# Reading two stages of matmul passes backwards, and changing the order of the three passes in two others

## The chip, the cores and the metric

One core of one Trainium2 chip runs the whole program. The metric is the device time of one execution in microseconds (us). The profile is a trace of one execution, on the five engines: TensorE (PE; its loads of the stationary operand are listed apart as PEld), VectorE (DVE), ScalarE (ACT), GpSimd (POOL) and SyncE (SP, which here only issues DMAs).

## What is computed

```python
scores = scale * q @ k^T - log(S)          # 4 batches, 12 heads, S = 448, head size 64
x = sigmoid(scores) @ v                    # joined to 1792 tokens x 768
x = square(relu(x @ moe_w_in)) @ moe_w_out # 768 -> 2048 -> 768
h = x @ moe2_w_in
out = (h * sigmoid(1.702 * h)) @ moe2_w_out
```

All inputs and outputs are float32.

## The kernel before

The program has an attention part (the first 128 us of the span) and then eight stages of one kind, in which the two feed-forward layers are computed. A stage is one of the four weight matrices for one half of the tokens: STAGES lists them as (layer, in or out, half), and stages 0, 1, 4, 5 multiply by an "in" matrix, stages 2, 3, 6, 7 by an "out" matrix. Every matrix product is done by a Strassen scheme of seven products P1 to P7, each cut into 8 units, so a stage has 56 units (UNITS) and the program 448.

A unit is three steps of [128 x 128] stationary by [128 x 448] moving (the list `pairs` in `product`). For accuracy each float32 operand is held as a high part and a low rest, both in the type fp32r, and a step is three matmuls ("passes") into one PSUM bank: high weights by high data (line 475), high weights by the rest of the data (line 476), low weights by high data (line 477). The weights are the stationary operand (tiles `s`, three of them in turn: `sh` is the high part, `lo` the low one), the data the moving one (tiles `t`: index 0 the high part, index 1 the rest). A stage thus has 56 x 3 x 3 = 504 passes, the eight stages 4032.

ACT writes the high parts of the weights (`s<-ld`, for two units at a time) and of the data (`t<-...`), DVE the low ones from them. SP brings the weight blocks from DRAM into `ld`. ACT and DVE also move finished PSUM banks out, and prepare the Strassen sums. The order of the instructions on every engine comes from a planner in the program: units on PE stand in a fixed order, the rest is placed by due times. The planner counts a unit as a whole (UNIT_US) and doesn't look into `go`, the function in `product` that issues the passes of one unit.

Each matmul instruction carries its own load of the stationary operand; the trace shows one load for every pass.

Of the kernel before, what the change touches and what calls it, by code (L numbers as in the profile page):

```python
# [16 lines left out]
B, H, S, D = 4, 12, 448, 64  # L17
# [15 lines left out]
UNITS = 7 * NF  # L33
# [44 lines left out]
WINDOW, URGENT = 0.25, 3.0  # L78

PACE = (6, 6, 5, 1, 4, 5, 5)  # L80


@with_exitstack
def sigmoid_attention_two_ffn(ctx: ExitStack, tc: tile.TileContext, qk, v, w, outT):
# [3 lines left out]
    nc = tc.nc  # L88
# [28 lines left out]
    mem = {"ps": ppool.tile([P, 8, 512], F32, name="ps")}  # L117
# [155 lines left out]
    turn, count = [0], [0]  # L273
# [190 lines left out]
    def product(unit, pairs, ready):  # L464
        sl = SL[unit // 2 % NSLOT]

        def go():
            sh, lo = sl[:, 0, unit % 2], sl[:, 1, unit % 2]
            if unit == 0:
                one = [nc.const_aps.tensor(1.0, [P, n], mybir.dt.bfloat16) for n in (P, D)]  # L470
                nc.tensor.matmul(mem["ps"][:, pairs[0][0], :D], *one, start=True, stop=True)  # L471
            for b, c, t, k, start, stop in pairs:
                cols = slice(c * P, (c + 1) * P)
                o = mem["ps"][:, b, :S]
                nc.tensor.matmul(o, sh[:, cols], t[:, 0, k], start=start, stop=False, skip_group_check=True)  # L475
                nc.tensor.matmul(o, sh[:, cols], t[:, 1, k], start=False, stop=False, skip_group_check=True)  # L476
                nc.tensor.matmul(o, lo[:, cols], t[:, 0, k], start=False, stop=stop, skip_group_check=True)  # L477

        units[unit].fn = go
        units[unit].need(lows[unit // 2], ready)  # L480
        for b in {b for b, *_ in pairs}:
            units[unit].need(*held.pop(b, ()))
# [181 lines left out]
    def settle():  # L664
# [16 lines left out]
        assert len(order) == len(Node.all)  # L681
        marks = [(0, 0.0), (PACE[0], pe_at[units[0]])]
        for st, count in enumerate(PACE[1:]):
            marks.append((marks[-1][0] + count, pe_at[units[(st + 1) * UNITS]]))
# [184 lines left out]
```

## Time and profile before

| | |
|---|---|
| Three timed runs | 951.08 us median, 950.97 to 951.43 |
| The profiled execution | 950.77 us, of which the span from first to last instruction is 949.0 us |
| PE, PEld, DVE, ACT busy | 100%, 87%, 85%, 64% of the span |
| Granted TensorE clock, mean | 1.000 |
| The 1344 passes of each of lines 475, 476, 477 | 29% of the chain that ended last, each |

A pass is listed with about 365 ns, though the next begins about 0.2 us after it: passes overlap in the array and their ends are modelled, so that the distance between two starts is what a pass costs, not its listed duration.

### The profile page before, as it was taken

To read this page: it belongs to the slowest core of one execution; us is meant where nothing else is said; L and a number is where in the kernel's file an instruction comes from. 1 tells how busy PE (TensorE), PEld (TensorE's weight loads), DVE (VectorE), ACT (ScalarE), POOL (GpSimd) and SP (SyncE) were. 2 spreads that over 40 slices of the span, in tenths; PEclk is the share of its full clock that TensorE was granted. 3 is DMA by queue.
4 is the path that set the end of the run, shared out by engine and by line. 5 is a ranking of instruction groups with operands and counts; after the bars stand their busy time and mean duration, and the time that the engine had idled before them with its cause. 6 is when DMAs were issued, how large, how long until landed. Compare 5 with 4: busy or idle time off the path is not lost.

```text
span 949.0 us, 13696 instructions
## 1 busy us (share of the span) xinstructions
PE 944.6 (100%) x4949; PEld 822.8 (87%) x4949; DVE 809.3 (85%) x839; ACT 604.6 (64%) x715; POOL 53.5 (6%) x100
## 2 busy tenths in 40 slices
PE   9999999999999999999999999999999999999998
PEld 4555479999999999999999999999999999999997
DVE  3989986699877999999999987999989999778662
ACT  6788776778868775555464666657684646445551
POOL 0110100000000000000000000000000000000000
PEclk9999999999999999999999999999999999999999
DMA  8899989999886766896567699877975448754341
GB/s 340 301 335 356 335 293 332 324 354 334 290 324 227 250 231 212 317 364 216 161 243 286 202 359 325 312 247 251 351 279 171 133 146 288 261 166 132 115 137 58
DMA packets 98627, 245.75 MB, mean 259 GB/s; under 512 B 10752, under 2 KB 72960, under 8 KB 94464
## 3 DMA queue, kind: packets, MB, share of 16 engines
q1 hardware_dynamic: 84736, 150.51, 46.5%
q0 software_dynamic: 13824, 94.38, 27.2%
q8 instruction: 38, 0.62, 0.3%
q14 instruction: 29, 0.24, 0.1%
HBM read 175.11 MB, written 69.73 MB: 258 GB/s over the span
## 4 chain that ended last, share of the span: by engine, by line
PE 100%; ACT 0%; issue 0%
PE ps L475 29%; PE ps L476 29%; PE ps L477 29%; PE ps L332 6%; PE ps L298 5%; PE ps L346 1%; PE ps L317 1%; PE ps L790 0%; PE ps L293 0%; ACT xq L635 0%; PE ps L471 0%
## 5 line engine op out<-in xcount | busy, mean ns | idle before, releaser
L475 PE MATMUL ps<-t,s 128*128 128x448 f32 x1344 | 490.9, 365 | 0.0
L477 PE MATMUL ps<-t,s 128*128 128x448 f32 x1344 | 490.8, 365 | 0.0
L476 PE MATMUL ps<-t,s 128*128 128x448 f32 x1344 | 490.8, 365 | 0.0
L153 ACT ACTIVATE s<-ld 128x768 fp32r<-128x768 f32 x224 | 189.4, 846 | 249.4 <-PE ps L476 206.6
L477 PEld LDWEIGHTS ps<-t,s 128*128 128x128 f32 x1344 | 252.5, 188 | 19.9
L476 PEld LDWEIGHTS ps<-t,s 128*128 128x128 f32 x1344 | 252.5, 188 | 19.9
L475 PEld LDWEIGHTS ps<-t,s 128*128 128x128 f32 x1344 | 252.5, 188 | 19.9
L156 DVE TENSOR_TENSOR s<-ld,s 128x768 fp32r<-128x768 f32 x224 | 213.6, 954 | 61.7 <-ACT s L153 56.6
L156 DVE TENSOR_TENSOR t<-h,t 128x1344 fp32r<-128x1344 f32 (+1 forms) x72 | 100.4, 1397 | 8.8 <-ACT t L153 8.7
L153 ACT ACTIVATE t<-h 128x1344 fp32r<-128x1344 f32 (+1 forms) x72 | 85.6, 1190 | 4.4 <-DVE h L156 2.9
L153 ACT ACTIVATE h<-ps 128x448 f32<-128x448 f32 x112 | 59.8, 536 | 27.0 <-PE ps L477 26.8
L153 ACT ACTIVATE a<-ps,bias 128x896 f32<-128x896 f32 x72 | 66.1, 1023 | 3.2 <-PE ps L293 3.2
L332 PE MATMUL ps<-a,rv 128*64 128x448 f32 x288 | 56.8, 543 | 0.1
L217 DVE SCALAR_TENSOR_TENSOR dec<-raw,dec 128x1536 uint32<-128x1536 uint32 x32 | 56.2, 1755 | 0.5
L219 DVE SCALAR_TENSOR_TENSOR dec<-raw,dec 128x1536 uint32<-128x1536 uint32 x32 | 56.1, 1753 | 0.3
L153 ACT ACTIVATE dec<-raw 128x1536 f32<-128x1536 f32 x32 | 51.9, 1621 | 0.0
L156 DVE TENSOR_TENSOR h<-h,h 128x1344 f32<-128x1344 f32 (+1 forms) x36 | 50.0, 1397 | 1.0 <-DMA h<-hm 0.8
L153 ACT ACTIVATE h<-h 128x896 f32<-128x896 f32 x48 | 44.9, 945 | 4.8 <-DVE h L156 4.4
L332 PEld LDWEIGHTS ps<-a,rv 128*64 128x64 f32 x288 | 19.6, 137 | 32.4 <-issue 22.6
L213 DVE TENSOR_SCALAR dec<-dec 128x1536 f32<-128x1536 f32 x32 | 30.7, 959 | 15.6 <-ACT dec L153 15.6
L156 DVE TENSOR_TENSOR t<-xq,t 128x1344 fp32r<-128x1344 f32 x24 | 37.2, 1552 | 5.9 <-ACT t L153 5.4
L156 DVE TENSOR_TENSOR h<-ps,h 128x448 f32<-128x448 f32 x64 | 38.8, 619 | 2.8 <-PE ps L477 2.5
(58 smaller groups left out, 616.1 us busy)
## 6 DMA issues: line engine op xcount, KB each, us to landing
ld<-scr SPq DMA_DIRECT2D x448, 192.0 KB, 3.8
raw<-in_w POOLq DMA_DIRECT2D x32, 1536.0 KB, 8.2
scr<-dec POOLq DMA_DIRECT2D x32, 768.0 KB, 5.5
scr<-raw POOLq DMA_DIRECT2D x28, 576.0 KB, 6.2
hm<-h SPq DMA_DIRECT2D x32, 448.0 KB, 5.8
h<-hm SPq DMA_DIRECT2D x16, 672.0 KB, 5.4
rq<-in_qk SPq DMA_DIRECT2D x22, 448.0 KB, 8.2
rv<-in_v SPq DMA_DIRECT2D x12, 448.0 KB, 6.1
```

The lines of the kernel that those rows point to most:

```text
L153: nc.scalar.activation(out, in_, fn, **kw)
L156: nc.vector.tensor_tensor(out=out, in0=in0, in1=in1, op=op)
L213: dve(lambda: nc.vector.tensor_scalar(out=d, in0=d, scalar1=LEAST, scalar2=LARGEST, op0=ALU.max, op1=ALU.min), 4 * W, [dk], each=0.52e-3)
L217: dve(lambda: nc.vector.scalar_tensor_tensor(out=u, in0=raw[:, :, 0], scalar=29, in1=u, op0=ALU.logical_shift_right, op1=ALU.bitwise_or), ...
L219: dve(lambda: nc.vector.scalar_tensor_tensor(out=u, in0=raw[:, :, 1], scalar=0x80000000, in1=u, op0=ALU.bitwise_and, op1=ALU.bitwise_or), ...
L298: nc.tensor.matmul(ps[:, j, :S], kk[rows, keys], qq[rows, QUERIES], start=(i == 0), stop=(i == 2))
L317: nc.tensor.matmul(ps[out, j, :S], r[rows, :LEFT], r[rows, QUERIES], start=True, stop=True)
L332: nc.tensor.matmul(ps[rows, :S], t[:, hp % 2 * NFULL + c, rows], a[:, j], start=(c == 0), stop=False)
L346: nc.tensor.matmul(mem["ps"][out, b + i, :S], t[rows, 2 * NFULL, out], AL[rows, j], start=False, stop=True)
L475: nc.tensor.matmul(o, sh[:, cols], t[:, 0, k], start=start, stop=False, skip_group_check=True)
L476: nc.tensor.matmul(o, sh[:, cols], t[:, 1, k], start=False, stop=False, skip_group_check=True)
L477: nc.tensor.matmul(o, lo[:, cols], t[:, 0, k], start=False, stop=stop, skip_group_check=True)
```

## The change

In `product`, stages 1 and 2 (TURNED: an "in" stage and an "out" stage) read the 448 columns of the moving operand from the last to the first, and write the 448 columns of the PSUM bank from the last to the first too. Each column of data still lands in its own column of the bank; all passes of these two stages are turned alike. In stages 4 and 5 (SWAPPED, both "in" stages) the third pass stands in second place: high by high, low weights by high data, high weights by the rest. The sums are the same but for the order of addition.

```diff
 PACE = (6, 6, 5, 1, 4, 5, 5)
+
+TURNED, SWAPPED = (1, 2), (4, 5)
...
+            turn = -1 if unit // UNITS in TURNED else 1
+
             for b, c, t, k, start, stop in pairs:
                 cols = slice(c * P, (c + 1) * P)
-                o = mem["ps"][:, b, :S]
-                nc.tensor.matmul(o, sh[:, cols], t[:, 0, k], start=start, stop=False, skip_group_check=True)
-                nc.tensor.matmul(o, sh[:, cols], t[:, 1, k], start=False, stop=False, skip_group_check=True)
-                nc.tensor.matmul(o, lo[:, cols], t[:, 0, k], start=False, stop=stop, skip_group_check=True)
+                o = mem["ps"][:, b, :S][:, ::turn]
+                hi, rest = t[:, 0, k][:, ::turn], t[:, 1, k][:, ::turn]
+                passes = [(sh, hi), (sh, rest), (lo, hi)]
+                if unit // UNITS in SWAPPED:
+                    passes = [passes[i] for i in (0, 2, 1)]
+                for i, (a, x) in enumerate(passes):
+                    nc.tensor.matmul(o, a[:, cols], x, start=start and i == 0, stop=stop and i == 2, skip_group_check=True)
```

On DVE, ACT, POOL and SP the instructions stand in the same order as before. On PE the same number of passes works on the same tiles; all of them now have one line, 484, and rows that read alike are drawn together with a count.

PE at the start of stage 4 (the first of the swapped ones), before. The names are the PSUM tile `ps`, the data tile `t` and the weight tile `s`, and in brackets stands the engine whose semaphore a pass waits for:

```order
L475 MATMUL ps_149<-t1_107,s1_116 128x448 [waits Activation_49]
L476 MATMUL ps_149<-t1_107,s1_116 128x448 [waits DVE_49]
L477 MATMUL ps_149<-t1_107,s1_116 128x448 [waits DVE_49]
L475 MATMUL ps_149<-t1_107,s1_116 128x448
L476 MATMUL ps_149<-t1_107,s1_116 128x448
L477 MATMUL ps_149<-t1_107,s1_116 128x448
```

The same place after:

```order
L484 MATMUL ps_149<-t1_107,s1_116 128x448 [waits Activation_49]
L484 MATMUL ps_149<-t1_107,s1_116 128x448 [waits DVE_49]
L484 MATMUL ps_149<-t1_107,s1_116 128x448 x16
L484 MATMUL ps_149<-t2_108,s2_117 128x448 [waits Activation_49]
L484 MATMUL ps_149<-t2_108,s2_117 128x448 [waits DVE_49]
L484 MATMUL ps_149<-t2_108,s2_117 128x448 x7
```

Before, the second pass waited for the rest of the data and the third for the low weights; now the second pass of a fresh weight tile waits for the low weights, and no wait stands at the third.

PE at the start of stage 1 (the first of the turned ones), before:

```order
L475 MATMUL ps_149<-t2_108,s1_116 128x448 [waits Activation_49]
L476 MATMUL ps_149<-t2_108,s1_116 128x448
L477 MATMUL ps_149<-t2_108,s1_116 128x448 [waits DVE_49]
L475 MATMUL ps_149<-t2_108,s1_116 128x448
L476 MATMUL ps_149<-t2_108,s1_116 128x448
```

The same place after:

```order
L484 MATMUL ps_149<-t2_108,s1_116 128x448 [waits Activation_49]
L484 MATMUL ps_149<-t2_108,s1_116 128x448
L484 MATMUL ps_149<-t2_108,s1_116 128x448 [waits DVE_49]
L484 MATMUL ps_149<-t2_108,s1_116 128x448 x6
L484 MATMUL ps_149<-t2_108,s1_116 128x448 [waits DVE_49]
```

Nothing moved here: the waits stand at the same passes, and the direction of the columns doesn't show in such rows.

## Rows read from the trace of the kernel before

**Rows 1.** The page: busy time of PE and PEld, share, instructions; granted clock.

```profile
PE 944.6 (100%) x4949; PEld 822.8 (87%) x4949; DVE 809.3 (85%) x839; ACT 604.6 (64%) x715; POOL 53.5 (6%) x100
...
PEclk9999999999999999999999999999999999999999
```

**Rows 2.** The page: the chain of work that ended last, by engine and line.

```profile
PE 100%; ACT 0%; issue 0%
PE ps L475 29%; PE ps L476 29%; PE ps L477 29%; PE ps L332 6%; PE ps L298 5%; PE ps L346 1%; PE ps L317 1%; PE ps L790 0%; PE ps L293 0%; ACT xq L635 0%; PE ps L471 0%
```

**Rows 3.** Groups by line: busy us, mean ns; idle us before them, who ended it.

```profile
L475 PE MATMUL ps<-t,s 128*128 128x448 f32 x1344 | 490.9, 365 | 0.0
L477 PE MATMUL ps<-t,s 128*128 128x448 f32 x1344 | 490.8, 365 | 0.0
L476 PE MATMUL ps<-t,s 128*128 128x448 f32 x1344 | 490.8, 365 | 0.0
L475 PEld LDWEIGHTS ps<-t,s 128*128 128x128 f32 x1344 | 252.5, 188 | 19.9
L476 PEld LDWEIGHTS ps<-t,s 128*128 128x128 f32 x1344 | 252.5, 188 | 19.9
L477 PEld LDWEIGHTS ps<-t,s 128*128 128x128 f32 x1344 | 252.5, 188 | 19.9
```

**Rows 4.** Stretches by stage, 0 to 7: busy us (instructions) by engine, clock, DMA.

```profile
core 0: us, PE busy (x) PEld busy (x) DVE busy (x) ACT busy (x) POOL busy (x), PEclk, DMA share, GB/s
128.06:230.28 102.22, 102.22 (x509) 94.76 (x506) 83.74 (x92) 72.11 (x97) 8.75 (x16) 1.00 0.93 329
230.28:332.42 102.14, 102.14 (x505) 94.68 (x504) 86.33 (x97) 79.67 (x106) 8.70 (x16) 1.00 0.78 277
332.42:434.57 102.15, 102.15 (x505) 94.68 (x504) 99.33 (x93) 59.85 (x62) 3.74 (x7) 1.00 0.81 286
434.57:536.72 102.15, 102.15 (x506) 94.68 (x505) 97.44 (x92) 56.74 (x56) 5.50 (x10) 1.00 0.62 208
536.72:638.86 102.14, 102.14 (x506) 94.67 (x504) 91.23 (x102) 66.72 (x88) 7.63 (x14) 1.00 0.88 309
638.86:741.00 102.14, 102.14 (x505) 94.68 (x504) 95.92 (x111) 64.03 (x89) 7.60 (x13) 1.00 0.74 259
741.00:843.14 102.14, 102.14 (x505) 94.68 (x504) 91.86 (x82) 56.88 (x60) 0.00 (x0) 1.00 0.61 202
843.14:945.30 102.16, 102.16 (x505) 94.49 (x503) 60.15 (x54) 45.82 (x48) 0.00 (x0) 1.00 0.36 114
```

**Rows 5.** Single passes in order of time, start of stage 1: start us, us.

```profile
230.28 0.36 PE L475 MATMUL ps<-t,s 128*128 128x448 f32 x1
230.49 0.36 PE L476 MATMUL ps<-t,s 128*128 128x448 f32 x1
230.69 0.36 PE L477 MATMUL ps<-t,s 128*128 128x448 f32 x1
230.89 0.36 PE L475 MATMUL ps<-t,s 128*128 128x448 f32 x1
231.09 0.37 PE L476 MATMUL ps<-t,s 128*128 128x448 f32 x1
```

**Rows 6.** The same view for PE's weight loads there.

```profile
230.29 0.19 PEld L476 LDWEIGHTS ps<-t,s 128*128 128x128 f32 x1
230.49 0.19 PEld L477 LDWEIGHTS ps<-t,s 128*128 128x128 f32 x1
230.69 0.19 PEld L475 LDWEIGHTS ps<-t,s 128*128 128x128 f32 x1
```

**Rows 7.** Weight loads of the bf16 passes at the very start.

```profile
1.11 0.15 PEld L790 LDWEIGHTS <-const-bfloat16-1.0 128*128 128x128 bf16 x1 [0.22 <-issue]
1.48 0.15 PEld L790 LDWEIGHTS <-const-bfloat16-1.0 128*128 128x128 bf16 x1 [0.23 <-issue]
1.85 0.15 PEld L790 LDWEIGHTS <-const-bfloat16-1.0 128*128 128x128 bf16 x1 [0.23 <-issue]
...
2.97 0.15 PEld L790 LDWEIGHTS <-raw 128*128 128x128 bf16 x1 [0.23 <-issue]
```

**Rows 8.** The chain in order of time, attention: start us, us, instructions.

```profile
19.96 4.73 PE ps L332 x24
```

**Rows 9.** DVE in stage 4: the low weights of units 38 and 39.

```profile
601.22 0.95 DVE L156 TENSOR_TENSOR s<-ld,s 128x768 fp32r<-128x768 f32 x1
```

**Rows 10.** PE there: the first three passes of unit 38 of stage 4.

```profile
606.02 0.37 PE L475 MATMUL ps<-t,s 128*128 128x448 f32 x1
606.23 0.36 PE L476 MATMUL ps<-t,s 128*128 128x448 f32 x1
606.43 0.36 PE L477 MATMUL ps<-t,s 128*128 128x448 f32 x1
```

**Rows 11.** ACT there: high weights, an earlier pair and units 38, 39.

```profile
595.08 0.85 ACT L153 ACTIVATE s<-ld 128x768 fp32r<-128x768 f32 x1 [1.07 <-PE ps L476]
...
599.39 0.84 ACT L153 ACTIVATE s<-ld 128x768 fp32r<-128x768 f32 x1
```

## Prediction

> **What bounds the kernel now.** I first read the busy shares and the granted clock: PE is busy for 944.6 us of a 949.0 us span, the clock at full level throughout [rows 1]. A busy PE alone proves little, because matmuls overlap, so next comes the chain of work that ended last. It is PE for 100%, and lines 475, 476 and 477, the three passes that the change edits, hold 29% each [rows 2]. The groups by line then say whether PE ever waits in them: the idle time before 4032 passes is 0.0 us [rows 3]. So PE's own pace sets the end, and anything that another engine does counts only if it makes PE wait.
>
> The pace has to be taken from starts. In the stretches by stage each stage takes 102.14 to 102.22 us [rows 4]; with 504 passes in one, a pass costs 102.14 / 504 = 0.2027 us. The single passes at the start of stage 1 agree: 230.28, 230.49, 230.69, 230.89, 231.09 [rows 5]. Seven stages lie within 0.02 us of each other, although DVE's load in them goes from 60 to 99 us, ACT's from 46 to 80 us and the DMA traffic from 114 to 309 GB/s [rows 4]. Whatever sets 0.2027 us is inside PE and its operand paths and doesn't care for the traffic of the others.
>
> What sets it isn't plain. 448 columns at the 2.4 GHz level, one a cycle, are 0.1867 us, so 0.016 us of each pass is something else. The load of the next stationary operand starts with the pass before it and takes 0.188 us [rows 3, 6], so that a load and a hand-over of some 0.015 us could be the bound just as well as the columns and a fixed cost of 0.016 us. I can't tell these apart from this trace. It matters below: by the first reading a small slowing of the columns is hidden under the load, by the second nothing of it is.
>
> **The sum is made against 950.77 us**, the profiled execution (span 949.0 us and 1.77 us around it); the median of the runs is 951.08 us, 0.31 us or 0.03% above it, and I carry changes over to the median as they are.
>
> **Part 1: swapped passes in stages 4 and 5** (1008 passes). Nothing is added or removed; what changes is who follows whom, the waits, and the releases.
>
> - Neighbours. Before, two passes in a row share their stationary operand (475 then 476), after it they differ in the middle, and instead two in a row share their moving operand. If sharing the weights saved anything, the step from 475 to 476 would be shorter than that from 476 to 477. It isn't: 0.21 and 0.20 us at the start of stage 1 [rows 5], 0.21 and 0.20 us in stage 4 [rows 10], and the loads are as many as the passes and equally long, 188 ns on each line [rows 3]. Sharing the moving operand is in the trace as well: in "out" stages line 477 of one step and 475 of the next read the same high data, and these stages take the same 102.14 to 102.16 us [rows 4]. Cost: 0.
> - Waits. The low weights are wanted one pass earlier, by 0.20 us. What covers this is DVE's lead. Over the 56 weight pairs of stages 4 and 5 the shortest lead is that of units 38 and 39 of stage 4: DVE ends them at 601.22 + 0.95 = 602.17 us [rows 9], the first pass on line 477 starts at 606.43 us [rows 10], 4.26 us later. It becomes 4.06 us. Cost: 0; without that cover it would be 0.20 us for each of 56 pairs, 11 us. The rest of the data is wanted one pass later, which can only help.
> - Releases. ACT's next high weights wait for the last pass that reads `sh`, now line 477's place instead of 476's, so such a wait (1.07 us in the row shown) ends 0.20 us later [rows 11]. Behind it in ACT's queue stand copies out of PSUM, and DVE's low weights follow it. The high weights of units 38 and 39 end at 599.39 + 0.84 = 600.23 us and are wanted at 606.02 us [rows 10, 11], a lead of 5.8 us, the shortest in these stages. Cost: 0, and what is late next is still PE itself.
>
> **Part 2: turned passes in stages 1 and 2** (1008 passes). No instruction, wait or load is added or moved; the stationary operand is loaded as before, and all passes on one bank go the same way, so a column is again added to one pass after it was written. The one question is the price of a descending step in a pass, reading SBUF and writing PSUM. No row of this trace has a descending operand on any engine. Each ns on a pass costs 1.008 us, since PE has no idle time to give [rows 3] and 1008 passes pay it. The bounds from the nearest rows:
>
> - Below: no pass can come faster than its load, 0.188 us [rows 3]: 1008 x (0.188 - 0.2027) = -14.8 us. No reason excludes that direction has a part in the unexplained 0.016 us, but nothing points to it.
> - Middle: 0, if a step of -1 goes like a step of +1.
> - Above: a pass whose columns go at half pace. Two rows show 448 columns at about half pace for other reasons: the bf16 passes at the start are (2.97 - 1.11) / 5 = 0.372 us apart [rows 7], and line 332 with plain float32 operands takes 4.73 us for 24 matmuls that run two at a time, 0.394 us for a pair [rows 8]. That is 1008 x (0.372 - 0.2027) = +170.7 us to 1008 x (0.394 - 0.2027) = +192.8 us.
>
> I take 0. The row it is nearest to is the pass itself: same type, shape, tiles and number of elements, 1792 bytes in one run in either direction. And if the load is the bound, up to some 0.015 us a pass stays hidden.
>
> One page bears on this. The trace shows only ascending passes, all at 0.2027 us [rows 4]. The Trainium skill, "SBUF — State Buffer", section "Door 1: The DMA port swizzle", says that SBUF is read in lines of 16 bytes and PSUM in lines of 8, that accesses staying in a line go at full pace, and that any PSUM pattern that isn't contiguous slows matmuls much. By its first half a descending run touches the same lines in pairs and costs 0; by its last half, read strictly, the turned passes are slow. No run so far shows which; the second is the first rival below.
>
> **Forecast:** 0 + 0 against the median, 951.1 us; if it holds, within 950 to 952.5.
>
> **The rivals.**
>
> 1. *Descending columns go at half pace* (slower). Place: the write into PSUM, or the read of `t`. If the hardware joins two neighbouring float32 columns into one access only when the address goes up, each column of a turned pass has an access of its own. It decides as soon as joining fails for either operand. For it: full pace is one column every 0.42 ns with an addition into PSUM for each, which leaves little room for single accesses. Against it: the addresses are as dense as before. Price: +171 to +193 us, 1122 to 1144 us; I put it at 1133 us. Chance 0.22; another 0.03 that it is worse than 1140 us.
> 2. *Descending columns cost a little* (slower): a few to some tens of ns in each pass, as for an address that starts at the far end. At 10 ns beyond what the load hides it is +10 us, at 90 ns +91 us, 961 to 1042 us. Chance 0.10.
> 3. *The changed order of passes makes PE wait* (slower): the shared weights are worth something after all, or a lead of 4 us is used up by DVE's low weights standing behind other work. Price: 0.20 us for each of 56 pairs, +11 us, 962 us. The leads speak against it. Chance 0.02.
> 4. *Descending columns are faster* (faster): the pass comes down to its load, -14.8 us, 936.3 us. Chance 0.05.
> 5. *The change does nothing*, because the turned read and the turned write are put back into ascending order when the program is built. The time is that of the forecast, and its chance is in it.
>
> **How the numbers follow.** About 0.2% (1.9 us) is what a measurement of this kernel can tell from no change. Within it: 0.58 (forecast and rival 5). Slower: 0.22 + 0.03 + 0.10 + 0.02 = 0.37. Faster: 0.05. The likeliest case holds less than 8 in 10, so the range goes on to rivals 2 and 3 and, since these give only 0.70 in all, to rival 1: 950 to 1140 us. Left out are the gain (0.05) and what lies above 1140 us (0.03 and the upper part of rival 1, about 0.04), some 0.12 in all. The likeliest case by itself is 950 to 952.5 us.
>
> **What would show it.** The stretches by stage are the test, because each edit has stages of its own: stages 1 and 2 at 102.1 us each mean that turning is free, 188 to 199 us each that rival 1 holds, 103 to 148 us rival 2, 94.8 us rival 4. Stages 4 and 5 should stay at 102.1 us and PE's idle time at 0.0; a wait of PE for DVE, or 108 us in one of them, would be rival 3. ACT's wait for `s` in stages 4 and 5 should end 0.20 us later against the first pass of its pair and nothing behind it should move PE. If stages 1 and 2 grow, the number of passes and the clock should be as before and DVE's and ACT's busy times spread over a longer stretch. The forecast is wrong above all if a descending step is no equal of an ascending one, of which this trace holds not one example.

## The result

The changed kernel takes 955.91 us (median of 4 runs, 955.35 to 957.64) against 951.17 us before: a ratio of 1.0053, 95% interval 1.0038 to 1.0067, slower by 4.7 us. The likeliest case of the prediction was no change, so the forecast itself failed; the time lies in the stated range. It has the form of the second rival (a small charge on each descending pass), but lies below the 961 us at which that rival's price began.

The profiled execution took 955.35 us with a span of 953.2 us. The page of the profile after, with the groups of the one line 484 that now holds all passes (busy us, mean ns, idle before), answers to [rows 1 to 3]:

```profile
PE 948.2 (99%) x4949; PEld 822.6 (86%) x4949; DVE 809.4 (85%) x839; ACT 604.6 (63%) x715; POOL 53.5 (6%) x100
...
PE 99%; DMA 1%; SPq 0%; ACT 0%; issue 0%; DVE 0%
PE ps L484 86%; PE ps L334 6%; PE ps L300 5%; PE ps L348 1%; PE ps L319 1%; DMA rq<-in_qk 1%; SPq L148 0%; ACT xq L642 0%; DVE qh L263 0%; PE ps L473 0%
...
L484 PE MATMUL ps<-t,s 128*128 128x448 f32 x4032 | 821.4, 366 | 0.0
L484 PEld LDWEIGHTS ps<-t,s 128*128 128x128 f32 x4032 | 757.3, 188 | 63.7
```

PE still sets the end and still never waits in the passes (0.0 us); the loads are as many and as long as before. The listed length of a pass went from 365 to 366 ns, which tells nothing. The stretches by stage tell it; the columns are the stretch and its length, busy us and instructions of PE, PEld, DVE, ACT and POOL, then clock, DMA share and GB/s:

```profile
128.28:230.51 102.23, 102.23 (x510) 94.77 (x507) 83.66 (x92) 71.93 (x97) 9.44 (x16) 1.00 0.93 329
230.51:334.66 104.15, 104.15 (x505) 94.67 (x504) 86.39 (x97) 79.95 (x107) 8.70 (x16) 1.00 0.77 271
334.66:438.82 104.16, 104.16 (x505) 94.67 (x504) 99.38 (x93) 60.05 (x62) 3.74 (x7) 1.00 0.80 281
438.82:540.97 102.15, 102.15 (x506) 94.68 (x504) 97.37 (x92) 56.72 (x56) 5.50 (x10) 1.00 0.61 208
540.97:643.11 102.14, 102.14 (x505) 94.68 (x504) 91.25 (x102) 66.35 (x88) 7.63 (x14) 1.00 0.88 308
643.11:745.25 102.14, 102.14 (x505) 94.68 (x504) 96.07 (x111) 64.06 (x88) 6.93 (x13) 1.00 0.74 259
745.25:847.40 102.15, 102.15 (x506) 94.68 (x504) 91.75 (x81) 56.82 (x61) 0.00 (x0) 1.00 0.61 202
847.40:949.54 102.14, 102.14 (x505) 94.49 (x503) 60.14 (x54) 45.81 (x48) 0.00 (x0) 1.00 0.36 114
```

Against [rows 4], stages 1 and 2, the turned ones, grew from 102.14 and 102.15 to 104.15 and 104.16 us, and nothing else moved. That is 2.01 us for 504 passes, 4.0 ns a pass, and 4.02 us in the two stages together. Of the 4.58 us between the two profiled executions the rest is some 0.22 us ahead of stage 0 (it begins at 128.28 instead of 128.06 us, with a load of q and k on the chain; in the runs below this start lies anywhere from 127.6 to 129.2 us) and some 0.34 us outside the span. The swapped stages 4 and 5 stand at 102.14 us to the hundredth.

### The profile page after: what moved, and what is told of

Same layout as the page of the kernel before. It is cut to its first block, busy times and chain, and to the rows that moved or that the text cites. A ratio compares the mean times of both kernels' runs of the same rounds, so it can differ in the third digit from the quotient of the medians.

```text
span 953.2 us, 13655 instructions
## 1 busy us (share of the span) xinstructions
PE 948.2 (99%) x4949; PEld 822.6 (86%) x4949; DVE 809.4 (85%) x839; ACT 604.6 (63%) x715; POOL 53.5 (6%) x100
## 4 chain that ended last, share of the span: by engine, by line
PE 99%; DMA 1%; SPq 0%; ACT 0%; issue 0%; DVE 0%
PE ps L484 86%; PE ps L334 6%; PE ps L300 5%; PE ps L348 1%; PE ps L319 1%; DMA rq<-in_qk 1%; SPq L148 0%; ACT xq L642 0%; DVE qh L263 0%; PE ps L473 0%
## 5 line engine op out<-in xcount | busy, mean ns | idle before, releaser
L484 PE MATMUL ps<-t,s 128*128 128x448 f32 x4032 | 821.4, 366 | 0.0
L148 POOL DMA_DIRECT2D scr<-dec x32 | 17.4, 545 | 404.0 <-DVE dec L158 404.0
L155 ACT ACTIVATE t<-xq 128x1344 fp32r<-128x1344 f32 x24 | 31.9, 1329 | 4.6 <-DVE xq L158 2.7
L158 DVE TENSOR_TENSOR raw<-dec 128x384 f32<-128x384 f32 x56 | 31.1, 555 | 1.0
L217 DVE TENSOR_SCALAR dec<-dec 128x1536 uint32<-128x1536 uint32 x32 | 30.6, 956 | 0.5
```

The source lines that it names most:

```text
L148: eng.dma_start(out() if callable(out) else out, in_() if callable(in_) else in_)
L155: nc.scalar.activation(out, in_, fn, **kw)
L158: nc.vector.tensor_tensor(out=out, in0=in0, in1=in1, op=op)
L217: dve(lambda: nc.vector.tensor_scalar(out=u, in0=u, scalar1=4, scalar2=1, op0=ALU.logical_shift_left, op1=ALU.logical_shift_right), 4 * W, ...
L484: nc.tensor.matmul(o, a[:, cols], x, start=start and i == 0, stop=stop and i == 2, skip_group_check=True)
```

## The experiments

Below, "pass" times are stage times divided by 504, as in the prediction. Up is ascending columns, down descending.

### Each edit alone, and turning everywhere

Three kernels, each with another line in place of the changed kernel's:

```diff
-TURNED, SWAPPED = (1, 2), (4, 5)
+TURNED, SWAPPED = (1, 2), ()
...
+TURNED, SWAPPED = (), (4, 5)
...
+TURNED, SWAPPED = (0, 1, 2, 3, 4, 5, 6, 7), ()
```

> Only the turned stages 1 and 2, passes in their old order everywhere. In the trace of the changed kernel stages 1 and 2 last 104.16 us each instead of 102.14, 4.0 ns more for each of 504 passes. Theory: turning alone is the whole cost of the change inside the stages, so these two stages read 104.16 us again, stages 4 and 5 102.14, and the time is 951.17 + 2 x 2.02 = 955.2 us. Rival: part of the 4.7 us between the medians comes from the swapped passes or from the start of the program (in the changed kernel's trace the attention part ends 0.22 us later, with PE waiting for the first loads of q and k); then this run is at 953 to 954.5 us.

Measured: 955.42 us, ratio 1.0042 (1.0029 to 1.0055), against 951.28 us for the kernel before beside it.

> Only the swapped passes of stages 4 and 5, no pass turned. Theory: 951.2 us, all eight stages at 102.14 to 102.23 us, PE without idle time. Rival: the swap costs what the turned passes don't explain of the difference between the medians, 4.7 - 4.0 = 0.7 us, so 951.9 us.

Measured: 951.43 us, ratio 1.0004 (0.9996 to 1.0013). The swap costs nothing that can be measured.

> All eight stages turned, no swap. Theory of a charge on every descending pass: 4032 x 4.0 ns = 16.1 us, 967.3 us, every stage at 104.16 us. Rival, a charge that depends on what stands beside it (the DMA traffic or DVE's load, which are lower in stages 6 and 7): stages differ, the later ones below 103.5 us, and the time is under 965 us.

Measured: 967.69 us, ratio 1.0171 (1.0155 to 1.0188); 16.4 us for 16.1 expected, and every stage from 1 to 6 within 104.15 to 104.17 us, whatever the traffic beside it. Stages 1 and 6:

```profile
233.20:337.35 104.15, 104.15 (x505) 94.67 (x504) 86.27 (x97) 79.77 (x106) 8.68 (x16) 1.00 0.78 270
753.98:858.15 104.17, 104.17 (x505) 94.67 (x505) 92.01 (x81) 56.95 (x60) 0.00 (x0) 1.00 0.61 198
```

So turning is the whole cost of the change in the stages, and it is paid pass by pass.

### Which side of a pass pays: reading SBUF or writing PSUM

From here to the run with fourteen places each kernel ran once, and only its stretches are read, all of them at a granted clock of 1.00. In this first one stage 0, read and written up, repeats the 102.22 us of [rows 4]. In the code shown `up` leaves the 448 columns as they are and `down` turns them; `skip(n)` takes every n-th column, in n rounds; `blocks(n)` takes blocks of n columns from right to left, ascending in each; `part(first, n, step)` takes n columns from `first` on, turned where the step is -1.

```diff
+READ_WRITE = (
+    (up, up), (down, up), (up, down), (down, down),
+    ((down, down), (up, up), (up, up)), ((up, up), (down, down), (up, up)),
+    (skip(2), up), (blocks(64), blocks(64)),
+)
...
+                    read, write = how[i] if len(how) == 3 else how
+                    nc.tensor.matmul(write(o), a[:, cols], read(x), ...
```

> By stage, columns read and written: 0 both up; 1 read down, written up; 2 read up, written down; 3 both down; 4 both down in the first pass of three only; 5 both down in the middle pass only; 6 read in steps of two (even columns, then odd), written up; 7 both in blocks of 64 columns, the blocks from right to left and the columns in each from left to right. Where a pass reads and writes in different orders the columns land in other places, so the values of stages 1, 2 and 6 are not the reference's; the work is the same. Theory, the PSUM write is what costs: stages 2 and 3 at 104.16 us, stage 1 at 102.14. Rival, the SBUF read costs: stages 1 and 3 at 104.16 us, stage 2 at 102.14. If both sides share it, both lie between. If a turned pass pays for itself, stages 4 and 5 each read 102.14 + 168 x 4.0 ns = 102.8 us; if meeting the column that was just written costs (a pass that begins where the one before it ended), they read more than 102.8 us, at 104 us or above. Stage 6 is 102.14 us if reads are only dearer when they go down, stage 7 is 102.14 us if a short jump back costs nothing, and above it if every jump back does.

The stretches of stages 1 to 7:

```profile
230.01:334.17 104.16, 104.16 (x506) 94.67 (x504) 86.39 (x97) 79.89 (x107) 8.68 (x16) 1.00 0.77 272
334.17:436.31 102.14, 102.14 (x505) 94.68 (x504) 99.22 (x93) 59.89 (x61) 3.72 (x7) 1.00 0.81 286
436.31:540.47 104.16, 104.16 (x506) 94.69 (x504) 97.79 (x92) 56.91 (x56) 5.48 (x10) 1.00 0.60 204
540.47:643.50 103.03, 103.03 (x505) 94.83 (x504) 91.10 (x102) 66.80 (x88) 7.61 (x14) 1.00 0.88 306
643.50:746.53 103.03, 103.03 (x505) 94.81 (x504) 95.97 (x111) 64.03 (x89) 6.92 (x13) 1.00 0.74 257
746.53:945.88 199.35, 199.35 (x506) 104.31 (x504) 93.26 (x82) 57.10 (x61) 0.00 (x0) 1.00 0.34 104
945.88:1048.05 102.17, 102.17 (x505) 94.51 (x503) 60.13 (x53) 45.64 (x48) 0.00 (x0) 1.00 0.35 112
```

Read down and written up (first row) costs the full 4.0 ns, read up and written down (second row) nothing, both down (third row) the same 4.0 ns. The read from SBUF pays; the theory that I had put first, the write, falls. With one turned pass of three (fourth and fifth row) it is 0.89 us for 168 turned passes, 5.3 ns each. That is more than the 4.0 ns of a charge that a pass pays for itself, and less than what meeting the column written last was expected to cost (104 us a stage or more). The starts of the single passes in this trace say more: in both stages a turned pass takes 203.3 ns to the next start, the ascending pass behind it 208.3 and the third 201.7 ns. Most of the charge thus falls on the pass behind the turned one; why, no run shows. The sixth row shows what an unlucky read costs: in steps of two columns 395.5 ns, near the 0.394 us with which the prediction bounded it. The last row, 64 columns up at a time with the blocks going down, is free, though every pass jumps back six times.

### Does the load of the weights set the pace, and is the charge by pass or by column

```diff
+READ_WRITE = tuple(
+    (part(0, n, step), part(0, n, step)) for n in (448, 384, 320, 224) for step in (1, -1)
+)
```

> Only the first columns of each pass are computed (the rest of the output is left as it was): 448, 384, 320 and 224 columns, each width in two stages, the first ascending, the second descending (stages 0 and 1: 448, 2 and 3: 384, 4 and 5: 320, 6 and 7: 224). Turned passes cost 4.0 ns at 448 columns, on the read side alone. Theory F, a fixed charge for a descending read: 4.0 ns at every width as long as the columns set the pace. Theory C, a charge by column (4.0 / 448 = 0.009 ns): 3.4 ns at 384, 2.9 at 320, 2.0 at 224. Beside it the pace of ascending passes: if the columns set it with 16 ns on top, 176 ns at 384, 149 ns at 320 and 109 ns at 224; if the load of the next stationary operand sets it (188 ns plus a hand-over), about 203 ns at every width, and direction shows no more below 448.

With narrow passes DVE and ACT fall behind and PE waits for them, so that whole stages can't be used (the run took 883.01 us). These are runs of passes without a wait: 384 columns up (199 passes), 384 down (124), 320 up (79), 320 down (75), 224 up (53), 224 down (159):

```profile
334.91:369.41 34.50, 34.50 (x201) 34.50 (x199) 34.47 (x33) 24.94 (x26) 0.54 (x1) 1.00 0.68 231
493.25:515.30 22.05, 22.05 (x125) 21.93 (x125) 21.91 (x22) 9.97 (x11) 2.14 (x4) 1.00 0.86 306
604.70:616.29 11.59, 11.59 (x82) 11.59 (x80) 11.59 (x15) 5.84 (x7) 1.07 (x2) 1.00 0.91 279
700.16:711.16 11.00, 11.00 (x77) 11.00 (x76) 10.90 (x15) 4.36 (x5) 0.53 (x1) 1.00 0.45 141
772.25:778.17 5.92, 5.92 (x54) 5.92 (x54) 5.92 (x6) 4.11 (x6) 0.00 (x0) 1.00 0.92 298
846.85:864.61 17.76, 17.76 (x161) 17.76 (x160) 16.84 (x16) 16.79 (x19) 0.00 (x0) 1.00 0.62 190
```

34.50 / 199 = 173.4 ns, 22.05 / 124 = 177.8, 11.59 / 79 = 146.7, 11.00 / 75 = 146.7, 5.92 / 53 = 111.7 and 17.76 / 159 = 111.7 ns. Loads of 128 x 128 weights, as large as ever, follow each other at 111.7 ns, so the 188 ns listed for a load are not what a load costs in a row, and the load does not set the 202.7 ns. The columns do, with 13.3 ns on top at 384 and 320 columns and 16.0 ns at 448. Direction costs 4.4 ns at 384 columns, about what it costs at 448, and nothing at 320: a fixed charge and a charge by column both fall (2.9 to 4.0 ns would show at 320). At 224 columns it costs nothing either, but there 18 ns lie on top of the columns, so that something else may set the pace and hide a charge.

### Is it the place where the read begins

```diff
+READ_WRITE = (
+    (part(0, 440), part(0, 440)), (part(1, 440), part(0, 440)), (part(2, 440), part(2, 440)), (part(3, 440), part(0, 440)),
+    *((part(first, 440, -1), part(first, 440, -1)) for first in (8, 6, 4, 2)),
+)
```

> 440 columns in every pass, the other 8 are left out. Stages 0 to 3 ascending, read from column 0, 1, 2, 3 (written from 0, 0, 2, 0); stages 4 to 7 descending, read and written from column 447, 445, 443, 441 down. Theory S, the charge comes from the place in a 16-byte group of four columns at which a read begins (a descending read of 448 begins at the last of a group): ascending reads from 1, 2 or 3 cost up to 4 ns more than from 0, and descending ones differ among themselves (447 and 443 are the last of a group, 445 and 441 the second). Rival, direction itself is charged: stages 0 to 3 are equal, stages 4 to 7 are equal and 4.0 ns a pass, 2.0 us a stage, above them.

The eight stretches; up from column 0, 1, 2, 3, then down from 447, 445, 443, 441:

```profile
129.16:230.04 100.88, 100.88 (x510) 94.74 (x506) 83.44 (x92) 71.67 (x97) 8.54 (x16) 1.00 0.93 331
230.04:334.19 104.15, 104.15 (x505) 96.01 (x504) 86.57 (x97) 79.87 (x107) 8.70 (x16) 1.00 0.78 272
334.19:435.00 100.81, 100.81 (x505) 94.63 (x504) 99.01 (x93) 59.99 (x61) 3.74 (x7) 1.00 0.82 289
435.00:534.12 99.12, 99.12 (x505) 95.19 (x504) 96.76 (x92) 56.69 (x56) 5.50 (x10) 1.00 0.64 216
534.12:634.92 100.80, 100.80 (x505) 94.75 (x504) 91.35 (x102) 66.84 (x88) 7.63 (x14) 1.00 0.89 312
634.92:737.40 102.48, 102.48 (x505) 95.51 (x504) 96.08 (x111) 64.14 (x89) 7.66 (x13) 1.00 0.73 258
737.40:838.20 100.80, 100.80 (x505) 94.75 (x504) 91.68 (x82) 56.80 (x60) 0.00 (x0) 1.00 0.62 204
838.20:941.24 103.04, 103.04 (x505) 96.40 (x503) 60.20 (x54) 45.76 (x48) 0.00 (x0) 1.00 0.35 113
```

A pass takes 200.2, 206.6, 200.0 and 196.7 ns going up and 200.0, 203.3, 200.0 and 204.4 ns going down. So at this width direction as such is not charged: 440 columns down from 447 cost what 440 up from 0 do. Going up, one column further at the start costs 6.4 ns (from 0 to 1) or saves 6.6 (from 1 to 2) or 3.3 ns (from 2 to 3).

### Jumps back, other steps, other loads

```diff
+READ_WRITE = tuple(
+    (blocks(n), blocks(n)) for n in (2, 4, 8, 16, 32, 64, 112, 224)
+)
```

> All 448 columns, read and written in blocks from right to left, ascending within a block; stages 0 to 7 have blocks of 2, 4, 8, 16, 32, 64, 112 and 224 columns. With 64 a pass was 202.7 ns, no dearer than straight. Theory F (a fixed charge for a descending innermost step): 202.7 ns in all eight. Theory J (each jump back costs, too little to be seen in 6 jumps): the dearer the smaller the block, with 224, 112 and 56 runs at blocks of 2, 4 and 8; if the reads go by groups of 16 bytes, blocks of 4 and more are free and blocks of 2 are near the 395 ns of a read in steps of two columns.

Measured, from the eight stretches: 206.8, 206.7, 206.6, 204.4, 204.0, 202.7, 205.0 and 204.0 ns a pass. Neither theory holds: it isn't 202.7 everywhere, and blocks of 112 and 224 columns, with three jumps back and one, are dearer than blocks of 64.

```diff
+READ_WRITE = (
+    (same, up), (skip(4), up), (skip(7), up), (lambda a: skip(2)(a)[:, ::-1, ::-1], up),
+    (up, up), (down, down), (lambda a: skip(2)(a)[:, :, ::-1], up), (up, up),
+)
+
+NARROW, FLIP = (4, 5), (7,)
```

> Reads in other steps, written ascending (values differ from the reference's where the order of the columns or the weights is changed). Stage 0 reads one column 448 times; 1 every fourth column; 2 every seventh; 3 every second column from right to left; 6 every second column upwards, the two halves each descending in pairs order; 4 and 5 load only 64 columns of weights in each pass, ascending in 4 and descending in 5; in 7 neighbouring passes take turns in direction, read and written. Read in steps of two columns a pass was 395.5 ns. If a read of SBUF takes a whole access for each column when neighbours aren't taken together, stages 1, 2, 3 and 6 are at 395 ns and stage 0 too; if accesses go by 16-byte groups, stage 1 and 2 are dearer than 395 ns and stage 0 is at 202.7 ns or less. If the load sets the pace of 202.7 ns, stage 4 with a load of about 137 ns falls to 188 or 189 ns; if the columns do, it stays at 202.7 and stage 5 at 206.7 ns. Stage 7 is at 204.7 ns if each turned pass costs 4.0 ns, at 205.3 ns or more if changing direction costs too.

Stages 0 to 5 (one column 448 times; every fourth; every seventh; every second, down; 64 columns of weights, up; the same, down):

```profile
129.14:224.56 95.42, 95.42 (x509) 95.34 (x506) 81.84 (x92) 70.37 (x96) 8.51 (x16) 1.00 0.95 342
224.56:427.82 203.26, 203.26 (x505) 104.73 (x505) 90.88 (x99) 82.51 (x108) 9.21 (x17) 1.00 0.43 151
427.82:621.03 193.21, 193.21 (x506) 104.33 (x505) 100.20 (x91) 60.21 (x62) 3.19 (x6) 1.00 0.44 145
621.03:825.98 204.95, 204.95 (x505) 104.78 (x504) 99.07 (x91) 56.55 (x57) 5.48 (x10) 1.00 0.31 108
825.98:927.93 101.95, 101.95 (x505) 67.39 (x504) 90.65 (x101) 66.56 (x88) 7.60 (x14) 1.00 0.84 298
927.93:1030.97 103.04, 103.04 (x505) 67.92 (x504) 96.05 (x111) 64.04 (x89) 6.92 (x13) 1.00 0.73 257
```

Reading one column again and again takes 95.42 / 504 = 189.3 ns, 2.7 ns above the 186.7 ns of its columns; of the 16 ns on top of an ordinary pass 13 come from walking through SBUF. Steps of two, four and seven columns up and of two down take about twice the time of a step of one, 383 to 407 ns (stage 6, the even columns from right to left and then the odd ones, lasts 204.94 us, as long as stage 3). Half the weights leave a pass at 202.3 ns up, once more not the load's pace, and 204.4 ns down. Directions in turn (stage 7) give 204.5 ns.

The page cited in the prediction ("SBUF — State Buffer" of the Trainium skill, section "Door 1: The DMA port swizzle") is not borne out here: by it, two float32 columns of a line of 16 bytes at a time, as in a step of two, go at full pace, and, read as strictly as the prediction read it, a PSUM bank written from right to left is slow. Measured, a step of two reads at 395.5 ns, and a bank written from right to left costs nothing.

```diff
+def weights(a, c, stage):
+    if stage < 2:
+        return a[:, c * P : c * P + 1].broadcast_to((P, P))
+    if stage < 4:
+        return a[:, 0 : 2 * P : 2]
+    if stage < 6:
+        return a[:, c * P : c * P + 32]
+    return a[:, 0:P]
```

> The moving read is whole, ascending in even stages and descending in odd ones; the load of the stationary operand is changed, so values are wrong: stages 0 and 1 load one column 128 times, 2 and 3 every second column, 4 and 5 only 32 columns, 6 and 7 the same 128 columns in every pass of a product's part. A pass that reads one column 448 times took 189.3 ns instead of 202.7, so some 13 ns come from where the moving operand is read. Theory L, the loads' reads of SBUF collide with the passes' own: with one column or 32 columns loaded the collisions are few, 189 to 192 ns in stages 0, 1, 4 and 5 and no difference between up and down. Theory N, the stalls are the moving read's own: 202.7 and 206.7 ns whatever is loaded.

One column of weights loaded 128 times, moving data up (first row) and down (second row); 32 columns of weights, up and down:

```profile
127.89:232.10 104.21, 104.21 (x509) 95.08 (x506) 83.98 (x92) 72.24 (x97) 8.52 (x16) 1.00 0.90 324
232.10:335.14 103.04, 103.04 (x505) 94.64 (x504) 86.21 (x97) 79.71 (x107) 8.69 (x16) 1.00 0.78 272
...
541.79:643.71 101.92, 101.92 (x506) 54.38 (x504) 91.00 (x102) 66.64 (x88) 7.61 (x14) 1.00 0.88 309
643.71:746.75 103.04, 103.04 (x506) 54.43 (x504) 96.07 (x111) 64.02 (x89) 6.92 (x13) 1.00 0.73 257
```

Here up is dearer than down, 206.8 to 204.4 ns, with the moving data in the same places as ever. What is loaded beside a pass therefore matters (theory N falls), but fewer loaded columns don't take the cost away (202.2 and 204.4 ns with 32; theory L as I put it falls too). With every second column loaded (stages 2 and 3) a pass takes 203.4 and 206.7 ns, and with the same 128 columns for all passes of a unit 202.7 and 206.7 ns.

### The place of the data in SBUF

```diff
-TURNED, SWAPPED = (1, 2), (4, 5)
+OFFSET, TURNED = (0, 1, 2, 3, 0, 1, 2, 3), (4, 5, 6, 7)
...
-    T = [cpool.tile([P, 2, NK, S], F32R, name=f"t{n}") for n in range(NT)]
+    T = [cpool.tile([P, 2 * NK * S + 4], F32R, name=f"t{n}") for n in range(NT)]
...
+            o = OFFSET[first // UNITS]
+            self.t = t = T[i][:, o : o + 2 * NK * S].rearrange("p (a k s) -> p a k s", a=2, k=NK)
```

> The data tiles begin 0, 1, 2 or 3 columns (0, 4, 8, 12 bytes) later in SBUF, with all 448 columns computed; stages 0 to 3 ascending with these four places in turn, stages 4 to 7 descending with the same four. (To make room, three weight buffers wait for DRAM instead of four; should PE wait for them, the pace is read from the passes that don't wait.) Theory D, direction itself costs 4.0 ns: 202.7 ns in stages 0 to 3, 206.7 in stages 4 to 7. Theory S, the place where a read begins decides: with 440 columns ascending reads from 0, 1, 2, 3 took 200.0, 206.7, 200.0 and 196.7 ns and descending ones from 447 no more than ascending ones from 0, so here stages 0 to 3 differ by several ns, about 202.7, 209, 203 and 199, and descending stages differ as much among themselves, one at least being no dearer than stage 0.

Measured: 204.5, 207.7, 205.8 and 201.1 ns going up, 205.3, 206.7, 206.7 and 209.6 ns going down. Even place 0 going up is not the 202.7 ns of [rows 4]. The padding had put the five data tiles at unlike places and moved the weights as well, so this run shows that places matter, and no more. The next one keeps them equal:

```diff
+FIRST_COLUMN = (0, 1, 2, 3, 4, 7, 8, 11, 12, 15, 16, 19, 20, 23)
...
+    T = [cpool.tile([P, 2 * NK * S + 64], F32R, name=f"t{n}") for n in range(NT)]
...
+            o, _ = place(first)
```

> The data tiles lie at equal places in groups of 256 bytes, as in the kernel before, and a product's operand begins some columns later in its tile: in the four out stages (2, 3, 6, 7) each of the seven products, 72 passes, has a place of its own. The places are 0, 1, 2, 3, 4, 7, 8, 11, 12, 15, 16, 19, 20 and 23 columns, ascending in stages 2 and 3 (seven places each) and descending in stages 6 and 7. In stages 0, 1, 4 and 5 the places are 0, 3, 7 and 11, all ascending. (Three weight buffers wait for DRAM instead of four, to make room.) So far data tiles 32 bytes apart from each other took 200.2 to 208.5 ns a pass ascending and 204 to 213 ns descending, with the weight tiles moved by 160 bytes too. Theory S: the place of the data alone moves the cost; place 0 gives 202.7 ns ascending and 206.7 descending, places 3, 7, 11, 15, 19 and 23 (the last column of a group of 16 bytes) about 200 ns ascending, place 1 above 205 ns, and the descending ones differ among themselves by several ns, some below 202.7. Theory W: it was the weights' place; then all ascending places give 202.7 and all descending ones 206.7 ns.

Some of the 28 stretches of 72 passes: up from place 1, 3, 8 and 16, then down from place 0, 3 and 23:

```profile
345.56:360.64 15.08, 15.08 (x74) 13.66 (x72) 14.25 (x14) 11.16 (x12) 0.00 (x0) 1.00 0.40 116
375.50:389.92 14.42, 14.42 (x73) 13.50 (x72) 14.27 (x14) 8.00 (x9) 0.00 (x0) 1.00 0.80 263
...
418.90:433.77 14.87, 14.87 (x73) 13.53 (x72) 11.34 (x10) 5.27 (x6) 0.53 (x1) 1.00 0.97 372
477.32:491.74 14.42, 14.42 (x74) 13.50 (x72) 14.35 (x16) 9.37 (x10) 1.22 (x2) 1.00 0.71 259
738.19:753.06 14.87, 14.87 (x73) 13.52 (x72) 14.84 (x16) 10.60 (x13) 0.00 (x0) 1.00 0.36 112
782.83:797.73 14.90, 14.90 (x74) 13.53 (x73) 13.88 (x14) 9.90 (x11) 0.00 (x0) 1.00 0.83 266
931.64:946.75 15.11, 15.11 (x73) 13.33 (x71) 3.81 (x4) 2.22 (x3) 0.00 (x0) 1.00 0.12 46
```

From the starts of the middle passes of each product, in ns:

| place (columns) | 0 | 1 | 2 | 3 | 4 | 7 | 8 | 11 | 12 | 15 | 16 | 19 | 20 | 23 |
|---|---|---|---|---|---|---|---|---|---|---|---|---|---|---|
| up | 202.7 | 209.8 | 206.5 | 200.2 | 202.2 | 200.3 | 206.7 | 201.7 | 202.9 | 200.2 | 200.0 | 200.3 | 203.3 | 201.2 |
| down | 206.7 | 206.7 | 206.7 | 206.7 | 206.7 | 206.7 | 206.7 | 206.7 | 206.7 | 206.7 | 206.7 | 206.7 | 206.7 | 210.0 |

Theory S holds for ascending passes: 200.0 to 209.8 ns by nothing but the place, the kernel before sitting at a middling one, and six of the seven best being those I had named (3, 7, 11, 15, 19, 23) with 16, which I had not. For descending passes it fails: they take 206.7 ns at 13 of 14 places. The in stages agree within 0.6 ns: at places 3, 7 and 11 a whole ascending stage averages 200.8, 200.7 and 201.8 ns. So the 4.0 ns of the change are the difference between the ascending price of place 0 and an almost constant descending one, and at places 1 and 8 a turned pass would not have been dearer at all.

### A version from it

```diff
-    T = [cpool.tile([P, 2, NK, S], F32R, name=f"t{n}") for n in range(NT)]
...
+    data = cpool.tile([P, NT * 2 * NK * S + 8], F32R, name="t")
+    T = [data[:, 3 + n * 2 * NK * S : 3 + (n + 1) * 2 * NK * S].rearrange("p (a k s) -> p a k s", a=2, k=NK) for n in range(NT)]
```

> The kernel before, with nothing turned or swapped, but all data tiles begin three columns (12 bytes) later in SBUF: the five tiles lie in one allocation with three columns ahead of the first. The order of instructions and waits on all engines is that of the kernel before. In the run with fourteen places an in stage at place 3 took 101.18 us and an out stage's product 200.2 ns a pass, so 100.9 us a stage, against 102.14 us. Theory S (the place of the moving data sets what SBUF adds to a pass): 4 x 0.96 + 4 x 1.22 = 8.7 us less, 942.5 us. Rival: the gain there came from what stood beside it (three weight buffers instead of four, tiles farther apart); then 951.2 us. A middle, if the places of the tiles among themselves matter too: 944 to 948 us.

Stages 1 and 2 of its trace:

```profile
229.67:330.84 101.17, 101.17 (x506) 94.77 (x504) 86.31 (x97) 79.57 (x107) 9.17 (x16) 1.00 0.79 279
330.84:431.75 100.91, 100.91 (x505) 94.54 (x504) 99.19 (x93) 59.73 (x61) 3.73 (x7) 1.00 0.82 289
```

Measured: 942.32 us, ratio 0.9902 (0.9885 to 0.9918) to the 951.45 us of the kernel before beside it. The eight stages add up to 808.45 us instead of 817.24. That is 1.0% faster than the kernel before and 1.4% faster than the changed one (942.32 / 955.91), with the same instructions in the same order and the moving data 12 bytes further on.

## Why the prediction was right or wrong

- **What bounds the kernel**: right. PE's pace is the time; every stage that changed did so by its passes, and PE waits for nothing in them.
- **Swapped passes cost 0**: right, by the run of them alone (ratio 1.0004) and by stages 4 and 5 at 102.14 us. The leads held: ACT's waits for `s` in the two stages grew from 40.3 us in 32 waits to 45.6 us in 36, the shortest lead of the low weights, of the same two units, became 3.86 us where 4.06 was worked out, and nothing came of it.
- **Turned passes cost 0**: this step failed. The term was 0 and measured 4.0 ns x 1008 = 4.0 us. I took the ascending pass as the nearest row because type, shape and number of elements are the same, and so assumed that these alone set the price of a read. The runs show that the address walk does too: 189.3 ns for one column, 200.0 to 209.8 ns for ascending walks from different places, 206.7 ns for descending ones from nearly all. That the read of SBUF and not the write of PSUM pays is shown; why a descending read is dearer is not.
- **The fixed 0.016 us that I couldn't explain** was the sign. I left it between a load and a fixed cost, with the load able to hide up to 0.015 us. The load is not the bound (111.7 ns a pass at 224 columns, so the listed 0.188 us was no floor), nothing is hidden, and some 13 ns of the 16 belong to the read of SBUF. A gain lay there as well, by moving the data and not by turning: 9.1 us over all 4032 passes, some 2.3 us for 1008, where I had bounded it at -14.8 us.
- **Rival 1, half pace**: fell for a step of -1 on both sides. Half pace exists for larger steps, at 383 to 407 ns against the 372 to 394 ns of its price; that neighbouring columns are joined into one access, as the rival pictured it, is not shown. The upper price was misread: the 0.394 us of [rows 8] spread the ends of a row over its 12 pairs, and inside it the pairs mostly start 0.376 us apart.
- **Rival 2, a small charge**: the one that came, at 4 ns where I had priced it at 10 to 90 ns. Its picture, an address that starts at the far end, is not the cause: 440 columns down from 447 cost what 440 up from 0 do.
- **The other rivals**: waits from the new order (3) fell with the run of the swap alone; a faster descending pass (4) and turned reads put back into order (5) fell with the 104.16 us of the turned stages.
- **The chances**: 0.58 on no change was too sure for an operand of which the trace had no example.

What stays open: why places and directions differ. That the loaded weights change which direction is dearer, and that one column of data without a walk takes 189.3 ns, speaks for two reads of SBUF, the pass's and the load's, falling in or out of step. This is argued, not shown: no run takes the load away, and loading 32 columns instead of 128 left a pass at 202.2 ns up and 204.4 down, which doesn't speak for it. Why descending passes of 448 columns cost 206.7 ns nearly everywhere and those of 384 are dearer too, while 440 and 320 columns go down as cheaply as up from some places, is not explained either, nor why most of a turned pass's charge falls on the pass behind it.

## What to carry to other kernels

When PE is the bound and never waits, divide a stage by its passes and compare with the columns: an unexplained rest of some ns a pass is worth an experiment on the address of the moving operand, since 8 bytes moved it by 9.6 ns here (places 1 and 3). Put several variants into one kernel, one for each stage or product, and read them from the stretches; that found in one run what whole-kernel times could not have told apart. Price an operand pattern that the trace doesn't show as unknown, however much it resembles the one that it shows.

## What the runs showed of the hardware

- A pass of 448 fp32r columns takes 200.0 to 209.8 ns ascending where only the place of its first column is changed, and 206.7 ns descending at 13 of 14 places; one column read 448 times takes 189.3 ns. What is loaded beside it moves this too: with one column of weights loaded 128 times it is 206.8 ns ascending and 204.4 ns descending.
- Steps of two, four and seven columns up, and of two down, in the read from SBUF take 383 to 407 ns for 448 columns.
- Writing a PSUM bank from right to left costs nothing (102.14 us a stage).
- A weight load is listed with 188 ns, yet passes with a load each follow each other at 111.7 ns when they have 224 columns.
